# Chunk 0 of a windowed attention with a two-layer network: scales of w_in found for two blocks at once instead of one

## The chip, the cores and the metric

One core of one Trainium2 chip runs the whole program. The metric is the device time of one execution in microseconds (us); three runs of the kernel before gave 936.11, 936.60 and 936.64 us, median 936.6.

## What is computed

Eight batches with eight heads, 576 positions and 64 channels go through causal attention with a window of 128 positions and a linear bias per head. The result, laid out as 4608 tokens by 512 channels, goes through two matrix products with a gate between them:

```python
scores = where((rel >= 0) & (rel < 128), q @ k.T / sqrt(64) - slope * abs(rel), -1e9)
attn = exp(scores - max(scores)); attn = attn / (sum(attn) + 1e-9)
x = (attn @ v).transpose(0, 2, 1, 3).reshape(4608, 512)
h = x @ w_in                                   # w_in 512 x 2048
g = where(h >= 1, h, where(h <= -1, 0, (h + 1) ** 2 / 4))
out = g @ w_out                                # w_out 2048 x 512
```

## The kernel before

The 4608 tokens are cut into 12 chunks of 384 (`CH`); a chunk has four pairs of heads (`p`, four a chunk). The columns of `w_in` and the rows of `w_out` are cut into 16 blocks of 128 (`fc`). For each chunk `c` and each block `fc`, `layer1` multiplies the chunk's `x` by block `fc` of `w_in` into a PSUM bank `h`, ScalarE makes `u` from it (L666), VectorE makes `g` (L667, L668), and `layer2`, two blocks later (`LAG`), adds `g` times the block of `w_out` to three accumulators `acc` (L688 in chunk 0, L691 to L693 in the others). Attention of later chunks is woven between these steps: `scores` (PE, tiles `s`), `soften` (VectorE L537, ScalarE L539, tiles `z`), sums and weights on GpSimd (L549, L550, tiles `ep`), `weights_t` (PE transposes, tiles `p`) and `values` (tiles `x`).

Numbers in fp32 are multiplied as two fp16 halves, high and low. So each block of `w_in` needs a power of two as its scale before it can be split. In chunk 0 this is done on the way, block by block:

- `fetch_weights` loads block `fc` of both matrices into one of three buffers `raw`; `unfold` (ScalarE L190, L191) and `float32_of` (VectorE L195) make them fp32 (`f_i` for w_in, `wf` for w_out). `convert_in` also reduces `f_i` to its largest magnitude per row (L204), `convert_out` does it for `wf` on ScalarE (L229).
- `scale_in` calls `scale_of`: PE spreads the column of row maxima over all partitions (`across`, L160, tile `m_i`), VectorE reduces it to one number (L167) and makes the power of two and its inverse by three operations on one column (L169, L170, L171), into `i_in` and `s_in`.
- `split_in` makes one more column operation (`fall_in`, L212) and then the halves of the block: ScalarE the high half (L220), VectorE the low one (L221), both named `wi`.

Which block is converted and which is scaled and split after which step `f` of layer 1 stands in two tables by hand, `CONVERT` and `SPLIT`; where a table has no entry, `f + 5` is converted and `f + 4` is split. The order on each engine is then set by the tile framework's scheduler, which works from the order of the code and the dependences it finds; each engine runs its own instructions strictly in that order.

The buffers that matter here: `h` has two PSUM banks (`ps_h`), the accumulators three, and all short-lived PSUM tiles (`s`, `p`, `x`, `m_i`) share three banks (`ps_a`). `f_i` has three buffers, `raw` three.

Of the kernel before, what the change touches and what calls it, by code (L numbers as in the profile page):

```python
# [15 lines left out]
ALU = mybir.AluOpType  # L16
# [4 lines left out]
def windowed_attention_then_ffn(  # L21
# [21 lines left out]
    V, S, G, T, DMA = nc.vector, nc.scalar, nc.gpsimd, nc.tensor, nc.sync  # L43
# [17 lines left out]
    X = mybir.AxisListType.X  # L61
# [15 lines left out]
    def bank(name):  # L77
        return ps_a.tile([P, 4 * P], F32, name=name, tag="ps_a")
# [61 lines left out]
    s_in = const.tile([P, NFC], F32, name="s_in")  # L140
    i_in = const.tile([P, NFC], F32, name="i_in")
# [3 lines left out]
    s_x, i_x, fall, gain, half, shift, o_g = {}, {}, {}, {}, {}, {}, {}  # L145
    tops, diag = {}, {}
    s_q, s_k, z_of, s_2, i_2 = {}, {}, {}, {}, {}

    def column(name, tag, bufs=2, n=1):
        return ap1.tile([P, n], F32, name=name, tag=tag, bufs=bufs)  # L150

    def spread(name, rows):

        diag[name] = rows

    def across(b, rows):

        r = rows.bitcast(BF16)
        for a in range(rows.shape[1]):
            T.matmul(b[:, a * P:(a + 1) * P], r[:, 2 * a + 1:2 * a + 2].broadcast_to([P, P]), ident16, start=True, stop=True)  # L160

    def scale_of(name, s, i):

        b = bank(f"m_{name}")[:, :P]
        across(b, diag.pop(name))
        top = column(f"top_{name}", "top")
        V.tensor_reduce(top, b, X, ALU.max)  # L167
        ti = top.bitcast(I32)
        V.tensor_scalar(ti, ti, 0x7F800000, None, ALU.bitwise_and)  # L169
        V.tensor_scalar(i, top, 2.0 ** -100, 1.0 / TOP, ALU.max, ALU.mult)  # L170
        V.reciprocal(s, i)  # L171
# [7 lines left out]
    def fetch_weights(fc):  # L179
        w = raw[fc] = rawp.tile([P, 2, DM, 2], I32, name=f"raw{fc}", tag=f"raw{fc % 3}")  # L180
        if 0 < fc < 3:
            G.memset(w[:1, :, 0, :1], 0)
        DMA.dma_start(w[:, 0].rearrange("p (c f) w -> p c f w", c=NCC),
                      wi32[:, 2 * fc * P:2 * (fc + 1) * P].rearrange("(c p) (f w) -> p c f w", p=P, w=2))
        DMA.dma_start(w[:, 1], wo32[fc * P:(fc + 1) * P, :].rearrange("p (f w) -> p f w", w=2))

    def unfold(fc, which=slice(0, 2)):

        low, high = raw[fc][:, which, :, 0], raw[fc][:, which, :, 1]
        S.activation(high.bitcast(F32), high.bitcast(F32), AF.Prelu, scale=2.0 ** -112, alpha=2.0 ** 32)  # L190
        S.activation(low, low.bitcast(U32), AF.Copy, scale=0.9375 * 2.0 ** -29)  # L191

    def float32_of(fc, a, out):

        V.scalar_tensor_tensor(out.bitcast(I32), raw[fc][:, a, :, 1], 3, raw[fc][:, a, :, 0], ALU.logical_shift_left, ALU.bitwise_or)  # L195

    wide, rows_i = {}, {}

    def convert_in(fc):
        f = wide[fc] = wp.tile([P, DM], F32, name=f"f_i{fc}", tag="f_i", bufs=3)  # L200
        unfold(fc)
        float32_of(fc, 0, f)
        rows = column(f"rows_i{fc}", "rows", 4)
        V.tensor_reduce(rows, f, X, ALU.max, apply_absolute_value=True)  # L204
        spread(f"i{fc}", rows)

    def scale_in(fc):
        s1, i1 = s_in[:, fc:fc + 1], i_in[:, fc:fc + 1]
        scale_of(f"i{fc}", s1, i1)

    def fall_in(fc):
        V.tensor_scalar(fall[0][:, fc:fc + 1], i_in[:, fc:fc + 1], i_x[0], 0.25, ALU.mult, ALU.mult)  # L212

    def split_in(fc):
        if fc > 1:
            fall_in(fc)
        f, s1 = wide.pop(fc), s_in[:, fc:fc + 1]
        t = wp.tile([P, 2, DM], F16, name=f"wi{fc}", tag=f"wi{fc}")
        wi[fc] = t.rearrange("p s (c f) -> p s c f", c=NCC)
        S.activation(t[:, 0], f, AF.Copy, scale=s1)  # L220
        V.scalar_tensor_tensor(t[:, 1], f, s1, t[:, 0], ALU.mult, ALU.subtract)  # L221
# [4 lines left out]
    def convert_out(fc):  # L226
        wf[fc] = wp.tile([P, DM], F32, name=f"wf{fc}", tag=f"wf{fc}")
        float32_of(fc, 1, wf[fc])
        S.activation(junk, wf[fc], AF.Abs, accum_out=rows_o[:, fc:fc + 1])  # L229

    def scale_out(stage):
        if stage == 0:
            V.tensor_reduce(rows_o[:, NFC:], rows_o[:, :NFC], X, ALU.max)
            spread("o", rows_o[:, NFC:])
        else:
            scale_of("o", s_out, i_out)
            V.tensor_reduce(reach, i_in, X, ALU.max)
            V.tensor_scalar(reach, reach, float(NCC * P) * TOP * TOP * 1.001, None, ALU.mult)
# [561 lines left out]
    for i in range(NCHUNK * NFC + LAG):  # L800
        c, fc = divmod(i, NFC)
        ops = []
        if c < NCHUNK:
            if i == 0:
                ops += [lambda g=g: split_x(0, g, xn.pop((0, g))) for g in range(NPAIR)]
            if c == 0 and fc == 0:

                ops.append(lambda: behind([last_x[0]], lambda: layer1(0, 0)))
            else:
                ops.append(lambda c=c, fc=fc: layer1(c, fc))  # L810
            if c == 0:
                ops.append(lambda fc=fc: convert_after(fc))
            if c == 0 and fc == NFC - 2:
                ops.append(lambda: scale_out(0))
            if c == 0 and fc == NFC - 1:
                ops.append(lambda: scale_out(1))
            if c == 1:
                ops.append(lambda c=c, fc=fc: behind(done_g[c, fc - 1] if fc else [], lambda: split_out(fc)))
            if fc == NFC - 1 and c + 1 < NCHUNK:
                ops.append(lambda c=c: scales(c + 1))  # L820
        ffn.append(ops)
        ops = []
        if i >= LAG:
            ops.append(lambda i=i: layer2(*divmod(i - LAG, NFC)))
        if c == 0:
            ops.append(lambda fc=fc: split_after(fc))
        ffn.append(ops)

    def convert_after(f):

        for fc in CONVERT.get(f, (f + 5,)):
            if fc < NFC:
                if fc + 2 < NFC:
                    fetch_weights(fc + 2)
                behind(done_g[f], lambda: convert_in(fc))
                behind(done_g[f], lambda: convert_out(fc))
        for fc in SPLIT.get(f, (f + 4,)):
            if fc < NFC:
                behind(done_g[f], lambda: scale_in(fc))

    def split_after(f):

        for fc in SPLIT.get(f, (f + 4,)):
            if fc < NFC:
                behind(done_g[f], lambda: split_in(fc))

    CONVERT = {0: (3,), 1: (4, 5), 2: (6,), 3: (7, 8)}
# [6 lines left out]
    def convert_early(t):  # L854
        m = EARLY[t]
        fc, second = divmod(t, 2)
        if not second:
            behind(done_t[m], lambda: fetch_weights(fc + 2))
        behind(done_t[m], lambda: (convert_out if second else convert_in)(fc))

    then = {4: [lambda: reach_of_v(0), lambda: reach_of_v(1)], 5: [lambda: scale_in(0), lambda: reach_of_v(2), lambda: reach_of_v(3)],
            6: [lambda: split_in(0), lambda: scale_x(0)], 7: [lambda: scale_in(1)],
            8: [lambda: split_in(1), lambda: fall_in(0), lambda: fall_in(1)]}
    keep_busy(KEEP[0])

# [59 lines left out]
```

## Time and profile before

| | |
|---|---|
| runs | 936.11, 936.60, 936.64 us |
| the profiled execution | 935.53 us |
| its span on the core | 933.8 us |
| PE / VectorE / ScalarE / GpSimd busy over the span | 97% / 73% / 68% / 24% |
| granted TensorE clock, mean | 0.992 of 2.4 GHz |

A busy share of PE is not a share of its peak: a matmul's record overlaps the next one's, so the tables of waits and the starts of neighbouring matmuls say more than the share. Engines are named PE (TensorE), DVE (VectorE), ACT (ScalarE) and POOL (GpSimd), and SP is the queue that issues most transfers. Chunk 0 runs from about 41 to 138 us of the span.

### The profile page before, as it was taken

What the parts mean: (1) busy time and instruction counts of PE and PEld (TensorE: products, weight loads), DVE (VectorE), ACT (ScalarE), POOL (GpSimd) and SP (SyncE); (2) the same over time, 40 slices, a digit from 0 to 9 for tenths busy, and PEclk for the clock granted to TensorE, in tenths of its full rate; (3) what the DMA queues carried; (4) which work ended last, traced back from release to release, by engine and by line L of the source; (5) the groups of instructions that cost most, each with busy time, mean ns of one, the idle gap of its engine ahead of it and who ended that gap; (6) DMA issues with size and microseconds to landing.
All of it is one profiled execution on the core that took longest, in us unless ns stands there. A gap on an engine that the chain in (4) does not pass through costs nothing.

```text
span 933.8 us, 18976 instructions
## 1 busy us (share of the span) xinstructions
PE 907.0 (97%) x6661; PEld 501.7 (54%) x6661; DVE 684.6 (73%) x2070; ACT 637.5 (68%) x1668; POOL 220.5 (24%) x298
## 2 busy tenths in 40 slices
PE   9789999999999999999999999999999999999997
PEld 6344554554555555555555555555555555555553
DVE  6889979988877876877877777777877867653332
ACT  5889958888677766676776677677677657643332
POOL 6332221211122212212222221221222221222221
PEclk9889999999999999999999999999999999999999
DMA  7657723444544343334344334424532412320001
GB/s 242 218 177 255 244 63 95 81 96 117 102 106 116 77 87 89 95 97 100 100 93 94 94 78 94 116 66 103 119 75 46 102 36 35 76 48 15 34 1 35
DMA packets 178736, 91.41 MB, mean 98 GB/s; under 512 B 128848, under 2 KB 168016, under 8 KB 178640
## 3 DMA queue, kind: packets, MB, share of 16 engines
q1 hardware_dynamic: 178496, 90.07, 38.8%
q8 instruction: 52, 0.85, 0.4%
q14 instruction: 44, 0.36, 0.1%
q10 hardware_dynamic: 144, 0.13, 0.0%
HBM read 49.28 MB, written 9.44 MB: 63 GB/s over the span
## 4 chain that ended last, share of the span: by engine, by line
PE 66%; DVE 18%; ACT 10%; issue 3%; DMA 1%; POOL 1%; DVEq 0%; SPq 0%; ACTq 0%; POOLq 0%
PE h L659 10%; PE h L660 10%; PE h L661 10%; PE acc L691 9%; PE acc L693 9%; PE acc L692 9%; PE x L629 3%; DVE g L667 3%; PE s L490 3%; PE acc L688 2%; ACT hl L585 2%; ACT z L511 2%; DVE g L668 2%; ACT u L666 2%; DVE z L509 2%
## 5 line engine op out<-in xcount | busy, mean ns | idle before, releaser
L676 POOL TENSOR_TENSOR gl<-g,gh 128x384 f16<-128x384 f32 x176 | 170.2, 968 | 608.6 <-ACT gh L675 552.6
L667 DVE SCALAR_TENSOR_TENSOR g<-u,half 128x384 f32<-128x384 f32 x176 | 112.0, 636 | 175.3 <-ACT u L666 172.6
L691 PE MATMUL acc<-wo,gh 128*128 128x512 f16 x528 | 200.4, 380 | 1.2 <-ACT o L704 1.1
L692 PE MATMUL acc<-wo,gh 128*128 128x512 f16 x528 | 200.1, 379 | 0.0
L693 PE MATMUL acc<-wo,gl 128*128 128x512 f16 x528 | 184.6, 379 | 0.3 <-POOL gl L676 0.3
L666 ACT ACTIVATE u<-h,shift,fall 128x384 f32<-128x384 f32 x176 | 115.8, 667 | 98.2 <-PE h L661 97.4
L675 ACT CAST gh<-g 128x384 f16<-128x384 f32 x176 | 89.6, 509 | 122.0 <-DVE g L668 111.3
L659 PE MATMUL h<-x,wi 128*128 128x384 f16 x384 | 125.3, 326 | 2.1 <-DVE g L668 1.7
L659 PE MATMUL h<-xh,wi 128*128 128x384 f16 x384 | 125.1, 326 | 2.2 <-DVE g L668 1.9
L660 PE MATMUL h<-x,wi 128*128 128x384 f16 x384 | 125.1, 326 | 0.5 <-DVE x L639 0.5
L660 PE MATMUL h<-xl,wi 128*128 128x384 f16 x384 | 125.2, 326 | 0.0
L661 PE MATMUL h<-x,wi 128*128 128x384 f16 x384 | 125.2, 326 | 0.0
L661 PE MATMUL h<-xh,wi 128*128 128x384 f16 x384 | 124.9, 326 | 0.0
L511 ACT ACTIVATE z<-z,nmax 128x192 f32<-128x192 f32 (+2 forms) x240 | 102.5, 430 | 16.8 <-DVE nmax L509 16.7
L668 DVE SCALAR_TENSOR_TENSOR g<-h,gain,g 128x384 f32<-128x384 f32 x176 | 108.4, 616 | 4.3
L660 PEld LDWEIGHTS <-wi 128*128 128x128 f16 x768 | 75.1, 98 | 62.7 <-issue 10.9
L659 PEld LDWEIGHTS <-wi 128*128 128x128 f16 x768 | 75.1, 98 | 58.9 <-issue 2.9
L661 PEld LDWEIGHTS <-wi 128*128 128x128 f16 x768 | 75.1, 98 | 51.2 <-issue 0.9
L586 DVE SCALAR_TENSOR_TENSOR hl<-z,rc,hl 128x192 f16<-128x192 f32 (+2 forms) x240 | 85.9, 413 | 7.5 <-ACT hl L585 6.6
L585 ACT ACTIVATE hl<-z,rc 128x192 f16<-128x192 f32 (+2 forms) x240 | 83.5, 430 | 3.5 <-DVE rc L518 2.4
L509 DVE CUSTOM_DVE_ANT_0 z<-s,near,z_of 128x192 f32<-128x192 f32 (+2 forms) x240 | 82.2, 393 | 3.6 <-PE s L490 3.5
L693 PEld LDWEIGHTS <-gl 128*128 128x128 f16 x528 | 51.6, 98 | 61.3 <-POOL gl L676 0.8
(159 smaller groups left out, 1221.4 us busy)
## 6 DMA issues: line engine op xcount, KB each, us to landing
out_dram<-o SPq DMA_DIRECT2D x35, 256.0 KB, 2.3
raw<-in_moe_w_in_dram SPq DMA_DIRECT2D x16, 512.0 KB, 4.5
raw<-in_moe_w_out_dram SPq DMA_DIRECT2D x16, 512.0 KB, 5.4
vn<-in_v_dram SPq DMA_DIRECT2D x32, 256.0 KB, 3.2
qk<-in_q_dram SPq DMA_DIRECT2D x40, 192.0 KB, 2.4
qk<-in_k_dram SPq DMA_DIRECT2D x28, 256.0 KB, 2.8
vn<-in_v_dram SPq DMA_DIRECT2D x16, 192.0 KB, 2.8
qk<-in_k_dram SPq DMA_DIRECT2D x12, 192.0 KB, 2.5
```

The lines of the kernel that those rows point to most:

```text
L511: d = S.activation(z[:, i, c0:KW], z[:, i, c0:KW], AF.Exp, bias=nmax[:, i:i + 1], scale=-1.0, accum_out=sm[:, i, 0:1])
L585: S.activation(hl[:, 0, i, w], z[:, i, c0:KW], AF.Copy, scale=rc[:, i:i + 1])
L659: T.matmul(ph, wi[fc][:, 0, cc, :], xh, start=(cc == 0), stop=False)
L660: T.matmul(ph, wi[fc][:, 0, cc, :], xl, start=False, stop=False)
L661: last_mm[0] = T.matmul(ph, wi[fc][:, 1, cc, :], xh, start=False, stop=(cc == NCC - 1)).ins
L666: first = S.activation(u, ph, AF.Relu, bias=shift[c] if c else quarter, scale=fall[c][:, col])
L667: V.scalar_tensor_tensor(g, u, half[c] if c else 0.5, u, ALU.min, ALU.mult)
L668: last = V.scalar_tensor_tensor(g, ph, gain[c][:, col] if c else fall[c][:, col], g, ALU.mult, ALU.max)
L676: G.tensor_tensor(gl, g, gh, ALU.subtract)
L691: T.matmul(a, gh[:, ts], wo[fc][:, 0], start=first, stop=False)
L692: T.matmul(a, gh[:, ts], wo[fc][:, 1], start=False, stop=False)
L693: last_mm[0] = T.matmul(a, gl[:, ts], wo[fc][:, 0], start=False, stop=last).ins
```

## The change

From block 2 on, an even block and the odd one after it share one `rows` tile of two columns, one `across` of two matmul passes into 256 columns, and one chain (reduce, mask, scale, reciprocal, `fall`) on two columns. The chain is therefore made when both blocks are converted, and both are split one after the other. `CONVERT` moves block 7 one step earlier (from step 3 to step 2); `SPLIT` now has an entry for each pair, at steps 0, 2, 3, 5, 7, 9 and 11. Blocks 0 and 1 are as before.

```diff
     def scale_of(name, s, i):
-        b = bank(f"m_{name}")[:, :P]
+        n = s.shape[1]
+        b = bank(f"m_{name}")[:, :n * P]
         across(b, diag.pop(name))
-        top = column(f"top_{name}", "top")
-        V.tensor_reduce(top, b, X, ALU.max)
+        top = column(f"top_{name}", "top", 2, n)
+        V.tensor_reduce(top, b.rearrange("p (a w) -> p a w", w=P), X, ALU.max)
...
         float32_of(fc, 0, f)
-        rows = column(f"rows_i{fc}", "rows", 4)
-        V.tensor_reduce(rows, f, X, ALU.max, apply_absolute_value=True)
-        spread(f"i{fc}", rows)
+        if fc < 2 or fc % 2 == 0:
+            diag[f"i{fc}"] = column(f"rows_i{fc}", "rows", 4, 1 if fc < 2 else 2)
+        rows = diag[f"i{fc}" if fc < 2 else f"i{fc - fc % 2}"]
+        V.tensor_reduce(rows[:, fc % 2 if fc > 1 else 0:][:, :1], f, X, ALU.max, apply_absolute_value=True)
 
     def scale_in(fc):
-        s1, i1 = s_in[:, fc:fc + 1], i_in[:, fc:fc + 1]
-        scale_of(f"i{fc}", s1, i1)
+        n = 1 if fc < 2 else 2
+        if fc < 2 or fc % 2 == 0:
+            scale_of(f"i{fc}", s_in[:, fc:fc + n], i_in[:, fc:fc + n])
 
     def fall_in(fc):
-        V.tensor_scalar(fall[0][:, fc:fc + 1], i_in[:, fc:fc + 1], i_x[0], 0.25, ALU.mult, ALU.mult)
+        n = 1 if fc < 2 else 2
+        V.tensor_scalar(fall[0][:, fc:fc + n], i_in[:, fc:fc + n], i_x[0], 0.25, ALU.mult, ALU.mult)
 
     def split_in(fc):
-        if fc > 1:
+        if fc > 1 and fc % 2 == 0:
             fall_in(fc)
...
-        for fc in SPLIT.get(f, (f + 4,)):
+        for fc in SPLIT.get(f, ()):
...
-    CONVERT = {0: (3,), 1: (4, 5), 2: (6,), 3: (7, 8)}
-    SPLIT = {0: (2,), 1: (3,), 2: (4, 5), 3: (6,), 4: (7, 8)}
+    CONVERT = {0: (3,), 1: (4, 5), 2: (6, 7), 3: (8,)}
+    SPLIT = {f: (n, n + 1) for f, n in zip((0, 2, 3, 5, 7, 9, 11), range(2, NFC, 2))}
```

The scheduler then places many instructions of chunk 0 and of the first third of chunk 1 anew. Line numbers of the changed kernel are 1 higher from L167, 3 higher from L204 and 4 higher from L212 on. Three places matter for the prediction.

**Place 1: the high halves of blocks 2 and 3 on ACT, early in chunk 0.** `wi2` and `wi3` are the high halves of the blocks, `z_10` and `z_11` the exponentials of the two heads of pair 5, `u_0_2` what follows layer 1 of block 2. Before:

```order
L229 ACTIVATE junk_159,rows_o_158<-wf5_737 128x512
L220 ACTIVATE wi2_693<-f_i2_540,s_in_153 128x512
L220 ACTIVATE wi3_768<-f_i3_614,s_in_153 128x512
L539 ACTIVATE z_10_754,sums_134<-z_10_754,nmax_10_755 128x256 x2
L539 ACTIVATE z_11_761,sums_134<-z_11_761,nmax_11_762 128x256 x2
L666 ACTIVATE u_0_2_804<-h_0_2_791,quarter_91,fall0_510 128x384
```

With the change:

```order
L233 ACTIVATE junk_159,rows_o_158<-wf5_739 128x512
L543 ACTIVATE z_10_749,sums_134<-z_10_749,nmax_10_750 128x256 x2
L543 ACTIVATE z_11_756,sums_134<-z_11_756,nmax_11_757 128x256
L441 ACTIVATE lus_160<-lus_160,qscale_97 128x384
L543 ACTIVATE z_11_756,sums_134<-z_11_756,nmax_11_757 128x256
L543 ACTIVATE z_11_756,sums_134<-z_11_756,nmax_11_757 128x192
L543 ACTIVATE z_10_749,sums_134<-z_10_749,nmax_10_750 128x192
L224 ACTIVATE wi2_693<-f_i2_540,s_in_153 128x512
L224 ACTIVATE wi3_696<-f_i3_614,s_in_153 128x512
L670 ACTIVATE u_0_2_795<-h_0_2_782,quarter_91,fall0_510 128x384
```

Six exponentials and the scaling of a query tile, all behind the scores of pair 5, now stand ahead of `wi2`.

The same place on PE, with `s_10` and `s_11` the scores of pair 5, `m_i` the spread row maxima and `h_0_2` layer 1 of block 2. Before:

```order
L160 MATMUL m_i3_740<-ident16_151,rows_i3_618 128x128
L462 MATMUL s_11_0_748<-kr_5_458,lus_160 128x256
L462 MATMUL s_10_0_747<-kr_5_458,lus_160 128x256
L462 MATMUL s_11_0_748<-kr_5_458,lus_160 128x256
L462 MATMUL s_10_0_747<-kr_5_458,lus_160 128x256
L659 LDWEIGHTS wi2_693
```

With the change:

```order
L466 MATMUL s_11_0_743<-kr_5_458,lus_160 128x256
L466 MATMUL s_10_0_742<-kr_5_458,lus_160 128x256
L466 MATMUL s_11_0_743<-kr_5_458,lus_160 128x256
L466 MATMUL s_10_0_742<-kr_5_458,lus_160 128x256
L160 LDWEIGHTS rows_i2_544
L160 MATMUL m_i2_622<-ident16_151,rows_i2_544 128x128
L466 MATMUL s_11_2_763<-kr_5_458,lus_160 128x192
L466 MATMUL s_10_2_762<-kr_5_458,lus_160 128x192
L160 LDWEIGHTS rows_i4_726
L160 MATMUL m_i4_823<-ident16_151,rows_i4_726 128x128
L160 LDWEIGHTS rows_1_688
L160 MATMUL m_x1_851<-ident16_151,rows_1_688 128x128
L663 LDWEIGHTS wi2_693
```

The scores now come ahead of the spreading of the row maxima (two passes), so the chain that gives `s_in` starts behind them.

**Place 2: PE behind layer 1 of blocks 10 and 11.** `p_14`, `p_15` are transposes of attention weights that POOL has just made, `x_7` the values of pair 7. The rows of before are those around the same transposes:

```order
L688 MATMUL acc_0_0_839<-wf11_1125,g_0_11_1439 128x512
L559 MATMUL p_14_1363<-ident_85,ep_14_1276 128x128 x3
L160 LDWEIGHTS rows_i14_1312
L160 MATMUL m_i14_1397<-ident16_151,rows_i14_1312 128x128
L559 MATMUL p_15_1404<-ident_85,ep_15_1283 128x128 x3
L688 MATMUL acc_0_1_840<-wf11_1125,g_0_11_1439 128x512
```

With the change:

```order
L665 MATMUL h_0_11_1365<-xh_0_3_589,wi11_1170 128x384
L160 LDWEIGHTS rows_i12_1143
L160 MATMUL m_i12_1265<-ident16_151,rows_i12_1143 128x128
L563 MATMUL p_14_1315<-ident_85,ep_14_1224 128x128 x3
L563 MATMUL p_15_1348<-ident_85,ep_15_1231 128x128 x3
L160 LDWEIGHTS rows_i14_1260
L160 MATMUL m_i14_1383<-ident16_151,rows_i14_1260 128x128
L692 MATMUL acc_0_0_835<-wf10_1005,g_0_10_1336 128x512
```

Before, layer 1 of blocks 12 and 13 and 2.3 rounds of layer 2 stood between block 11 and `p_14`; now `p_14` follows block 11, and blocks 12 and 13 come after both transposes.

**Place 3: DVE at the end of chunk 0.** `g_0_14` at L668 is the last reader of the PSUM bank that `h_1_0`, the first layer 1 of chunk 1, is written to; `vs`, `h_8`, `h_9` and `wo0` are low halves of values, queries and keys, and w_out. Before:

```order
L667 SCALAR_TENSOR_TENSOR g_0_14_1568<-u_0_14_1567 128x384
L371 TENSOR_SCALAR s_k2_1491<-i_q2_1487,s_22_1545 128x4
L376 TENSOR_SCALAR near_133<-near_133,s_22_1545 128x192
L423 TENSOR_SCALAR r2_2747<-r2_2747 128x1
L668 SCALAR_TENSOR_TENSOR g_0_14_1568<-h_0_14_1554,fall0_510,g_0_14_1568 128x384
L445 SCALAR_TENSOR_TENSOR vs_8_1763<-vn_8_993,s_22_1545,vs_8_1763 128x512
```

With the change:

```order
L250 SCALAR_TENSOR_TENSOR wo0_1633<-wf0_403,s_out_155,wo0_1633 128x512
L390 SCALAR_TENSOR_TENSOR h_8_1521<-qk_8_961,s_k2_1435,h_8_1521 128x512
L431 TENSOR_SCALAR half2_2695<-u2_2692 128x1
L432 TENSOR_SCALAR shift2_2696<-u2_2692 128x1
L436 TENSOR_SCALAR o_g2_2694<-o_g2_2694,i_out_156 128x1
L433 TENSOR_SCALAR fall1_850<-i_in_154,i_x1_849,shift1_1558 128x16
L390 SCALAR_TENSOR_TENSOR h_9_1751<-qk_9_971,s_k2_1435,h_9_1751 128x512
L671 SCALAR_TENSOR_TENSOR g_0_14_1512<-u_0_14_1511 128x384
L434 TENSOR_SCALAR gain1_1555<-fall1_850,half1_1557 128x16
L671 SCALAR_TENSOR_TENSOR g_0_15_1540<-u_0_15_1539 128x384
L672 SCALAR_TENSOR_TENSOR g_0_14_1512<-h_0_14_1498,fall0_510,g_0_14_1512 128x384
```

Three `vs`, `wo0`, `h_8` and `h_9`, six operations of 512 columns, now stand ahead of `g_0_14`; before, they stood behind it or, `wo0`, much later.

## Rows read from the trace of the kernel before

**Rows 1.** The profile's page: busy time of each engine over the span, and the granted clock by 40 equal slices.

```profile
PE 907.0 (97%) x6661; PEld 501.7 (54%) x6661; DVE 684.6 (73%) x2070; ACT 637.5 (68%) x1668; POOL 220.5 (24%) x298
PEclk9889999999999999999999999999999999999999
```

**Rows 2.** Busy time by stretch; columns: stretch, its length, then busy us and instructions of PE, weight loads, DVE, ACT and POOL, granted clock, DMA share, GB/s.

```profile
70.00:95.00 25.00, 23.34 (x108) 11.96 (x105) 22.60 (x67) 22.41 (x47) 6.06 (x13) 1.00 0.75 264
95.00:120.00 25.00, 25.00 (x133) 13.55 (x132) 24.12 (x73) 22.70 (x46) 9.50 (x15) 1.00 0.70 222
120.00:145.00 25.00, 24.68 (x145) 13.03 (x144) 18.35 (x74) 13.91 (x30) 3.71 (x10) 1.00 0.22 64
```

**Rows 3.** Timeline of PE: the starts at which it waited between 60 and 164 us; columns: start, length, engine, line, operation, tiles, shape, count, and in brackets the idle time and what ended it.

```profile
65.28 2.84 PE L688 MATMUL acc<-wf,g 128*128 128x512 f32 x6 [0.19 <-DVE g L668]
68.96 0.23 PE L160 MATMUL m_i<-ident,rows_i 128*128 128x128 bf16 x1 [0.84 <-DVE rc L545]
70.83 2.84 PE L688 MATMUL acc<-wf,g 128*128 128x512 f32 x6 [0.19 <-DVE g L668]
78.69 0.23 PE L160 MATMUL m_i<-ident,rows_i 128*128 128x128 bf16 x1 [0.36 <-DVE rows_i L204]
80.03 0.32 PE L659 MATMUL h<-xh,wi 128*128 128x384 f16 x1 [1.11 <-DVE g L668]
138.16 0.32 PE L659 MATMUL h<-x,wi 128*128 128x384 f16 x1 [0.32 <-DVE g L668]
163.31 0.90 PE L629 MATMUL x<-lus,vs 128*64 128x256 f16 x14 [1.83 <-DVE rc L517]
```

**Rows 4.** Waits of PE between 200 and 270 us: who waited for whom, us in total, times, longest.

```profile
PE acc L691 <- ACT o L704: 1.1, 1, 1.1
PE h L659 <- DVE g L668: 1.0, 2, 0.6
PE h L660 <- DVE x L639: 0.5, 1, 0.5
```

**Rows 5.** Timelines around place 1, PE first, then ACT, then DVE; columns as in rows 3.

```profile
58.38 0.22 PE L160 MATMUL m_i<-ident,rows_i 128*128 128x128 bf16 x1
58.53 1.13 PE L462 MATMUL s<-kr,lus 64*128 64x256 f32 x8
59.59 0.34 PE L659 MATMUL h<-xh,wi 128*128 128x384 f16 x1
...
61.65 0.59 PE L462 MATMUL s<-kr,lus 64*128 64x192 f32 x2
...
56.99 0.71 ACT L220 ACTIVATE wi<-f_i,s_in 128x512 f16<-128x512 f32 x1
...
57.73 0.75 DVE L221 SCALAR_TENSOR_TENSOR wi<-f_i,s_in,wi 128x512 f16<-128x512 f32 x1 [1.06 <-ACT wi L220]
```

**Rows 6.** Groups of instructions between 50 and 145 us; columns: line, engine, operation, tiles, shape, count, then busy us and the mean ns of one, then the idle time before them.

```profile
L537 DVE CUSTOM_DVE_ANT_0 z<-s,rel 128x256 f32<-128x256 f32 x6 | 2.5, 420 | 0.0
L537 DVE CUSTOM_DVE_ANT_0 z<-s,rel 128x192 f32<-128x192 f32 x6 | 2.0, 354 | 0.5 <-PE s L462 0.4
L539 ACT ACTIVATE z<-z,nmax 128x256 f32<-128x256 f32 x12 | 5.9, 495 | 0.0
L539 ACT ACTIVATE z<-z,nmax 128x192 f32<-128x192 f32 x6 | 2.7, 450 | 0.6 <-DVE nmax L537 0.6
L437 ACT ACTIVATE lus<-lus,qscale 128x384 f32<-128x384 f32 x2 | 1.2, 616 | 1.6 <-PE s L462 1.6
L167 DVE TENSOR_REDUCE top_i<-m_i 128x1 f32<-128x128 f32 x14 | 3.8, 283 | 0.0
L366 DVE TENSOR_REDUCE i<-m 128x2 f32<-128x256 f32 x1 | 0.4, 418 | 0.0
L169 DVE TENSOR_SCALAR top_i<-top_i 128x1 int32<-128x1 int32 x14 | 2.0, 147 | 0.0
L170 DVE TENSOR_SCALAR i_in<-top_i 128x1 f32<-128x1 f32 x14 | 1.9, 146 | 0.1
L171 DVE RECIPROCAL s_in<-i_in 128x1 f32<-128x1 f32 x14 | 2.0, 156 | 0.2
L212 DVE TENSOR_SCALAR fall<-i_in,i_x 128x1 f32<-128x1 f32 x14 | 2.6, 196 | 0.0
L445 DVE SCALAR_TENSOR_TENSOR vs<-vn,s,vs 128x512 f16<-128x512 f32 x3 | 2.1, 741 | 0.0
```

**Rows 7.** Granted clock: a stretch at the lower level (columns as in rows 2), and what PE waited for as the level fell (columns as in rows 3).

```profile
48.20:54.90 6.70, 5.23 (x10) 2.52 (x11) 6.70 (x14) 6.70 (x10) 1.96 (x4) 0.50 0.21 62
...
49.08 1.69 PE L559 MATMUL p<-ident,ep 128*128 128x128 f32 x6 [2.71 <-POOL ep L550]
```

**Rows 8.** Timeline around place 2: ACT and DVE idle in chunk 0's last quarter, POOL ahead of `p_14`; columns as in rows 3.

```profile
123.08 0.67 ACT L666 ACTIVATE u<-h,quarter,fall 128x384 f32<-128x384 f32 x1 [3.85 <-PE h L661]
...
123.78 0.56 DVE L667 SCALAR_TENSOR_TENSOR g<-u 128x384 f32<-128x384 f32 x1 [3.15 <-ACT u L666]
...
116.65 2.02 POOL L549 TENSOR_TENSOR z<-z 128x384 f32<-128x384 f32 x2 [8.14 <-ACT z L539]
118.74 1.93 POOL L550 TENSOR_TENSOR ep<-z,rc 128x384 f32<-128x384 f32 x2
```

More of the change, by code (lines that the diff above doesn't have):

```diff
@@ L841, in split_after @@
     def split_after(f):
-        for fc in SPLIT.get(f, (f + 4,)):
+        for fc in SPLIT.get(f, ()):
             if fc < NFC:
                 behind(done_g[f], lambda: split_in(fc))
-    CONVERT = {0: (3,), 1: (4, 5), 2: (6,), 3: (7, 8)}
-    SPLIT = {0: (2,), 1: (3,), 2: (4, 5), 3: (6,), 4: (7, 8)}
+    CONVERT = {0: (3,), 1: (4, 5), 2: (6, 7), 3: (8,)}
+    SPLIT = {f: (n, n + 1) for f, n in zip((0, 2, 3, 5, 7, 9, 11), range(2, NFC, 2))}
     EARLY = (2, 3, 4, 5, 6, 7)
```

## Prediction, before the changed kernel was run

> **What bounds the kernel now.** I read the busy shares first: PE is busy for 97% of the span, VectorE (DVE) for 73%, ScalarE (ACT) for 68% [rows 1]. So only what PE waits for, or the speed at which it runs, can move the time by much. The clock line beside them shows full speed but for two early slices [rows 1]. Then I read the stretches of chunk 0, which is all that the change rewrites: DVE is busy for 22.6 and 24.1 of 25 us, ACT for 22.4 and 22.7, and PE, at full clock, for 23.3 and 25.0 [rows 2]. All three are nearly full there, and one can't tell from shares who holds up whom. The starts at which PE waits decide it: in chunk 0 behind 60 us there are six, 0.19, 0.84, 0.19, 0.36, 1.11 and 0.32 us, 3.0 us together, and one of 1.83 early in chunk 1 [rows 3]. DVE ended all of them, but they are all the time that PE can win back there. Between 200 and 270 us a further 1.1 + 1.0 + 0.5 = 2.6 us of waits stand [rows 4].
>
> The profiled execution took 935.5 us, the median of the runs is 936.6: sums are made against the profile, and 1.1 us is added at the end. A difference under 0.2% (1.9 us) can't be told from none.
>
> **What it removes.** A pair saves one reduce, one mask, one scale, one reciprocal and one `fall`, 35 instructions over seven pairs. By durations a pair gives back 2 x 0.283 - 0.418 (the reduce of 2x128 that stands elsewhere in the kernel) + 0.147 + 0.146 + 0.156 + 0.196 = 0.79 us [rows 6], 5.6 us of DVE in all. A record's length contains time that overlaps the next one, so this is the upper end. The lower end is nothing for what lies in a dependent chain, where a second column was done while the first chain's results were on their way; half, 2.8 us, is what I take for DVE's own time. For PE I price it at nothing where DVE waits for somebody else: at the first pair it does (below), and in the last quarter of chunk 0 DVE stands idle for 3.15 us and ACT for 3.85 us, waiting for PE [rows 8]. If that cover is gone, it is worth at most the waits named above.
>
> The Trainium skill ("Perfetto Trace Analysis", section Optimizing Scalar/DVE Operations) puts a fixed cost of about 60 ns on a DVE instruction that reads SBUF and about 125 ns on one that reads PSUM, and says that grouping helps where the engine is saturated. By it the saving would be an estimated 28 x 0.06 + 7 x 0.125 = 2.6 us of DVE; the sum goes by the rows.
>
> **Place 1, the first pair.** Before, ACT splits block 2 from 56.99 to 57.70, DVE makes the low half by 58.48, and layer 1 of block 2 (`h_0_2`) starts at 59.59, right behind the scores that start at 58.53, without a wait [rows 5]. Now the spreading of the row maxima stands behind those scores. I walk it: the scores start where `m_i3` stood, at 58.38, and take 59.59 - 58.53 = 1.06 us, to 59.4; two passes of `m_i2` end at about 59.7. DVE has the softening of pair 5 and the chain on its list, and ACT has six exponentials and the scaling of the query tile ahead of `wi2`. The first exponential can start one softening (0.42) after the scores, at 60.1; four exponentials of 0.495, two of 0.45 and the scaling of 0.616 make 3.5 us [rows 6]; then the high half at 0.71 [rows 5] ends at 64.3. So `h_0_2` starts at 64.3 where it started at 59.6, 4.7 us later. Between stand only the 192-column scores (0.59 [rows 5]), `m_i4` and a share of `m_x1`, 0.9 to 1.1 us: PE waits for **+3.6** more. Bounds: 3.1 if ACT's neighbours overlap, 4.0 if the low half queues too. DVE's saving is worth nothing here, since it is ACT's list that is late.
>
> **The clock.** In the profile of before the granted clock was 0.50 from 48.2 to 54.9 us, that is 1.2 instead of 2.4 GHz, and PE had waited 2.71 us at 49.08 and had been idle ahead of it too [rows 7]. The new wait at place 1 is longer than that one. If the clock falls behind it for the same 6.7 us, PE does half the work in it and loses 3.35; if not, nothing. Nearest row: the fall beside a wait of 2.7. I take a fall, and **+2.3**, since about 1 us of it is time in which PE would have waited for the next splits anyway.
>
> **Old waits between 65 and 81 us.** PE comes to them 3 to 6 us later, and what it waited for there (`g`, `rc`, `rows_i` of DVE) is not behind the late split, so they go: 0.19 + 0.84 + 0.19 + 0.36 + 1.11 [rows 3], **-2.7**. Ends: 0 and -2.7.
>
> **Place 2, behind block 11.** `p_14` and `p_15` wait for POOL's two sums and two weightings, 2.02 + 1.93 = 3.95 us of work that starts at 116.65 in before and ends at 120.7 [rows 8]. Before, layer 1 of blocks 12 and 13 and rounds of layer 2 stood ahead of `p_14`; now PE comes to it right behind block 11. POOL can't start sooner by as much, as its exponentials and the reciprocals `rc` stand behind the row maxima of block 12 and of `x_1` on DVE. Adding up the new lists from the previous common point, PE is through with block 11 at 118.7 and POOL with the last weighting at 121.0, on the clock of before. Bounds 0 (POOL moves up with it) and 3.95 (PE waits for all four); I take **+2.3**. Queued behind the waiting transposes is layer 2 of block 10, so nothing covers it. DVE's and ACT's own idle time of 3 us [rows 8] shrinks by it, which costs nothing.
>
> **Place 3, the end of chunk 0.** Layer 1 of chunk 1 writes a bank whose last reader is `g_0_14`. Six low halves of 512 columns now stand ahead of it, 0.74 us each [rows 6], 4.4 us in all; PE has about half of that in other work before it (layer 2 of blocks 13 and 14, pieces of attention). With the old wait of 0.32 [rows 3] gone in it, **+2.0**; bounds 0 and 4.4.
>
> **Later.** These low halves are then done early, so the wait of 1.83 at 163.31 for `rc` [rows 3] loses its reason: **-1.8** (ends 0 and -1.8). Of the 2.6 us of waits behind 200 us [rows 4] a PE that is some 6 us late finds half made: **-1.3** (ends 0 and -2.6). SP issues the same transfers; the one that refills the buffer of block 5 waits for `f_i5`, now some 7 us later, and no wait of PE in [rows 3] was put down to a transfer, so I cost that at nothing; its cover is the weaving of the attention, and without it place 2 would grow.
>
> **Sum:** 3.6 + 2.3 - 2.7 + 2.3 + 2.0 - 1.8 - 1.3 = +4.4, so 939.9 for the profile and **941.0** for the median.
>
> **A rule for the same point.** The same section of the Trainium skill says that where Scalar and Vector aren't saturated but cause bubbles on other engines, instructions broken up may let work end sooner. That is this change read backwards. The trace agrees as to before: with single columns `h_0_2` waited for nothing [rows 5].
>
> **Rivals.**
> 1. *DVE is the bound in chunk 0, and its saved time comes through* (the other side). For it: 24.1 of 25 us busy [rows 2], and DVE ends every wait of PE behind 60 us [rows 3]. Then the 3.0 us of chunk 0 and the 1.83 go: 936.6 - 4.8 = 931.8. It decides if the first pair's wait stays under about 1 us, that is if `wi2` comes out ahead of the exponentials at run time. Against: each engine keeps its list's order, and the list has them ahead. 0.15.
> 2. *No fall of the clock.* All as forecast without the 2.3: 938.7. For it: at 49 us more than one wait came together, at place 1 it is one. 0.23.
> 3. *Nothing is given back.* The fall at its full 3.35, the later 1.3 not absorbed: 941.0 + 1.05 + 1.3 = 943.4. For it: behind 200 us PE has had some waits for ACT's `o` [rows 4] which a shift of all engines together leaves as they are. 0.12.
>
> **How the numbers follow.** The forecast has 0.50, with its own range of 938.5 to 943.0 from the bounds of places 2 and 3, of which 0.08 may fall under 938.5. Slower: 0.42 of it, 0.11 of rival 2 and the 0.12 of rival 3, 0.65. Within 0.2%: 0.08 + 0.12 of rival 2 + 0.02 of rival 1, 0.22. Faster: 0.13. The range, 935.5 to 944.5, leaves out nearly all of rival 1 and a little at the top.
>
> **What would show it.** Right: `h_0_2` starts near 64 instead of 59.6 with a wait of 3 to 4 us for ACT's `wi`; a stretch at clock 0.50 within the next 10 us; a wait of `p` for POOL's `ep` near 120; a wait of `h` for `g` near 145 in place of 0.32; the 1.83 of `x` gone; 35 DVE instructions fewer. Wrong: a wait at place 1 under 1 us with the clock at 1.00 throughout (rival 1), or PE waits behind 92 us that sum to what they were.

## The result, and the profile after

Five runs of the change gave 940.99 to 942.41 us, median 941.58; five of before gave a median of 936.6. The ratio is 1.0059 (95% interval 1.0049 to 1.0070): slower by 5.5 us (4.6 to 6.6) by the ratio, by 5.0 between the medians. The forecast was 941.0, range 935.5 to 944.5, slower. The profiled execution took 942.41 us with a span of 940.7, 6.9 us over the span of before.

The page of the change, busy times and granted clock, beside [rows 1]:

```profile
PE 913.2 (97%) x6661; PEld 503.1 (53%) x6661; DVE 685.9 (73%) x2035; ACT 638.5 (68%) x1668; POOL 221.5 (24%) x298
PEclk9689999999999999999999999999999999999999
```

35 VectorE instructions fewer, and VectorE is busy for 1.3 us more. The chains take 2.7 us less (9.6 against 12.3, below), but other instructions take longer: the 16 conversions to `f_i` last 0.84 us each where they lasted 0.72, 1.7 us in all, in both profiles of either kernel. Why they do is open. TensorE's work is the same, and the span is longer.

The starts at which PE waited for over 0.15 us between 58 and 165 us, columns as in [rows 3]:

```profile
62.21 0.93 PE L466 MATMUL s<-kr,lus 64*128 64x192 f32 x4 [0.82 <-DVE top_i L168]
66.16 0.34 PE L663 MATMUL h<-xh,wi 128*128 128x384 f16 x1 [2.37 <-ACT wi L224]
67.75 0.50 PE L665 MATMUL h<-xh,wi 128*128 128x384 f16 x1 [0.16 <-DVE wi L225]
72.76 2.84 PE L692 MATMUL acc<-wf,g 128*128 128x512 f32 x6 [0.33 <-DVE g L672]
85.00 2.84 PE L692 MATMUL acc<-wf,g 128*128 128x512 f32 x6 [0.22 <-DVE g L672]
100.95 2.84 PE L692 MATMUL acc<-wf,g 128*128 128x512 f32 x6 [0.46 <-DVE g L672]
123.94 0.55 PE L563 MATMUL p<-ident,ep 128*128 128x128 f32 x3 [1.83 <-POOL ep L554]
124.72 0.83 PE L563 MATMUL p<-ident,ep 128*128 128x128 f32 x3 [0.24 <-POOL ep L554]
125.99 3.95 PE L692 MATMUL acc<-wf,g 128*128 128x512 f32 x6 [0.26 <-DVE g L672]
139.13 2.84 PE L692 MATMUL acc<-wf,g 128*128 128x512 f32 x6 [0.17 <-DVE g L672]
150.51 0.32 PE L663 MATMUL h<-x,wi 128*128 128x384 f16 x1 [0.96 <-DVE g L672]
```

ScalarE at place 1:

```profile
61.85 0.51 ACT L543 ACTIVATE z<-z,nmax 128x256 f32<-128x256 f32 x1 [3.04 <-DVE nmax L541]
...
65.40 1.32 ACT L224 ACTIVATE wi<-f_i,s_in 128x512 f16<-128x512 f32 x2
```

The six exponentials and the query's scaling run from 61.85 to 65.40 without a gap, and only then `wi2`. At place 1 `h_0_2` waits 2.37 us for `wi2` of ScalarE, at place 2 the transposes wait for POOL's `ep`, at place 3 `h_1_0` waits for `g_0_14`. The wait of 1.83 at 163.31 has no row any more. Between 200 and 280 us, beside [rows 4] (the stretch is longer at its end, since the same matmuls come 7.5 to 9.5 us later here):

```profile
PE h L663 <- DVE g L672: 1.0, 2, 0.6
PE acc L695 <- ACT o L708: 0.4, 1, 0.4
```

Stretches of the change at the lower clock, 1.2 GHz, columns as in [rows 2]:

```profile
25.90:42.60 16.70, 13.18 (x51) 6.70 (x53) 14.24 (x50) 13.13 (x30) 5.33 (x10) 0.50 0.72 249
53.10:56.60 3.50, 3.50 (x5) 1.42 (x6) 3.50 (x7) 3.50 (x6) 0.22 (x1) 0.51 0.29 83
66.80:70.80 4.00, 3.84 (x14) 1.63 (x15) 3.96 (x4) 0.01 (x1) 2.82 (x4) 0.57 0.00 0
124.90:128.60 3.70, 3.44 (x8) 1.67 (x8) 3.70 (x11) 2.54 (x8) 3.06 (x8) 0.55 0.56 189
```

The third stretch lies behind the wait of place 1, the fourth behind that of place 2. The first two begin ahead of the first instruction that the change moves on any engine (54.12, on VectorE); the second stands where before has the stretch of [rows 7], and is shorter.

### The profile page after: what moved, and what is told of

The parts are those of the page before. It is cut to its first block, busy times and chain, and to the rows that moved or that the text cites. A ratio compares the mean times of both kernels' runs of the same rounds, so it can differ in the third digit from the quotient of the medians.

```text
span 940.7 us, 18940 instructions
## 1 busy us (share of the span) xinstructions
PE 913.2 (97%) x6661; PEld 503.1 (53%) x6661; DVE 685.9 (73%) x2035; ACT 638.5 (68%) x1668; POOL 221.5 (24%) x298
## 4 chain that ended last, share of the span: by engine, by line
PE 64%; DVE 18%; ACT 13%; issue 3%; POOL 1%; DMA 0%; DVEq 0%; ACTq 0%; SPq 0%; POOLq 0%
PE h L663 10%; PE h L665 10%; PE h L664 10%; PE acc L695 9%; PE acc L696 9%; PE acc L697 9%; PE x L633 3%; DVE g L671 3%; ACT hl L589 3%; PE s L494 2%; DVE g L672 2%; ACT z L515 2%; ACT u L670 2%; DVE z L513 2%; PE acc L692 2%
```

## The experiments

The theory: TensorE is held up at named places, because the order of the lists was changed; a wait in place 1 or 2 also brings down the clock; VectorE's saved time is worth nothing there. Each ratio below is to runs of before on the same chip.

| run | us | ratio, 95% interval |
|---|---|---|
| e1, pairs from block 4 on | 939.1 | 1.0021 (1.0011 to 1.0030) |
| e2, first pair alone | 940.98 | 1.0054 (1.0037 to 1.0071) |
| e3, single columns, new tables | 936.88 | 1.0000 (0.9992 to 1.0009) |
| e4, pairs, first split at step 1 | 938.67 | 1.0022 (1.0012 to 1.0032) |
| e5, place 1 filled with matmuls | 945.68 | 1.0094 (1.0080 to 1.0109) |
| e6, saved time put back | 943.04 | 1.0069 (1.0056 to 1.0082) |
| e7, pairs split a step earlier | 935.73 | 0.9998 (0.9990 to 1.0007) |
| e8, as e4, last two pairs earlier | 937.16 | 1.0015 (1.0007 to 1.0024) |
| e9, before again, one run | 936.32 | |
| e10, the change again, one run | 946.35 | |
| e11, the change, last two pairs earlier | 940.98 | 1.0048 (1.0035 to 1.0062) |
| e12, the chain by single columns | 943.87 | 1.0070 (1.0056 to 1.0084) |

### Which part of the change costs the time: e1 and e2

e1 keeps blocks 2 and 3 single:

```diff
-        n = 1 if fc < 2 else 2
+        n = 1 if fc < 4 else 2
...
-    SPLIT = {f: (n, n + 1) for f, n in zip((0, 2, 3, 5, 7, 9, 11), range(2, NFC, 2))}
+    SPLIT = {0: (2,), 1: (3,), **{f: (n, n + 1) for f, n in zip((2, 3, 5, 7, 9, 11), range(4, NFC, 2))}}
```

> Blocks 2 and 3 keep single columns and steps 0 and 1; pairs from block 4 on, at the steps of the change. TensorE's list is that of before up to block 3 and that of the change from block 4 on. Theory (place 1 and the clock behind it carry most of the loss): h_0_2 waits for nothing near 59.6 us, the clock stays at full speed behind it, places 2 and 3 stay: 936.5 to 938.0, some 4 to 5 us under the change. Rival (the loss is made at places 2 and 3): 940 to 941.5, as the change. Rival (saved VectorE time is worth something once place 1 is out of the way): under 935.

e2 pairs blocks 2 and 3 alone:

```diff
-        n = 1 if fc < 2 else 2
+        n = 1 if fc not in (2, 3) else 2
...
+    SPLIT = {0: (2, 3), 1: (), 2: (4, 5), 3: (6,), 4: (7, 8)}     # and f + 4 behind, CONVERT of before
```

> Only blocks 2 and 3 are a pair, at step 0; all others single, by the tables of before. Theory: place 1 waits as in the change (2.4 us for wi of ScalarE, with what lies around it 3.5), the clock falls for some 4 us behind it, places 2 and 3 are as before: 939 to 941. Rival (places 2 and 3 carry the loss): 936 to 937.5.

The wait of place 1 is there in e2 as in the change, with the row that PE waits at first:

```profile
61.52 0.93 PE L466 MATMUL s<-kr,lus 64*128 64x192 f32 x4 [0.82 <-DVE top_i L168]
65.47 0.34 PE L663 MATMUL h<-xh,wi 128*128 128x384 f16 x1 [2.71 <-ACT wi L224]
```

and in e1 it is gone, while those of places 2 and 3 stand:

```profile
120.92 0.55 PE L563 MATMUL p<-ident,ep 128*128 128x128 f32 x3 [1.84 <-POOL ep L554]
...
146.54 0.32 PE L663 MATMUL h<-x,wi 128*128 128x384 f16 x1 [0.96 <-DVE g L672]
```

One pair of seven costs 5.1 us by e2's ratio; the other six cost 2.0 by e1's. Together that is 1.6 more than the 5.5 that the change loses by its ratio. The intervals would allow no difference, but e1's trace shows a wait and a stretch at the lower clock that neither before nor the change has:

```profile
72.86 0.86 PE L563 MATMUL p<-ident,ep 128*128 128x128 f32 x3 [2.09 <-POOL ep L554]
```

```profile
72.90:76.40 3.50, 3.50 (x7) 1.95 (x8) 3.19 (x5) 3.47 (x10) 1.42 (x3) 0.51 0.07 25
```

In the change TensorE is late enough from place 1 to come to these transposes at 77.24 without a wait. So part of what is late at place 1 covers what would be late behind. e1 was expected under 938.0, with the clock at full speed behind `h_0_2`; it is 1.1 over, and this wait and this fall are what I had not listed. e2's time came out as expected, but its place 3 is not as before: `h_1_0` waits 1.36 us there.

### Pairing or the steps: e3 and e4

e3 is the kernel before with both tables of the change; e4 is the change with `CONVERT` of before and the pairs at other steps:

```diff
-    SPLIT = {f: (n, n + 1) for f, n in zip((0, 2, 3, 5, 7, 9, 11), range(2, NFC, 2))}
+    SPLIT = {f: (n, n + 1) for f, n in zip((1, 2, 4, 5, 7, 9, 11), range(2, NFC, 2))}
```

> Both tables of the change, but every block by a column of its own, with the 35 small operations back. Theory (the place of the split decides, not the number of small operations): wi2 and wi3 stand ahead of the exponentials of pair 5, so no wait at place 1; 936 to 939, faster than the change. Rival (the saved small operations are worth their 3 us of VectorE, and the steps cost what the change costs): 943 to 945.

> All pairs kept, CONVERT as before, the first pair's split at step 1 and the third's at step 4; by the list the spread row maxima of blocks 2 and 3 then stand ahead of the scores of pair 5, and the tail from block 4 on is the change's. Theory: no wait of h_0_2 for ScalarE over 1 us, so 936.5 to 938.5 with all the pairs. Rival (a pair's chain costs its wait wherever it stands, since the first block waits for the second's conversion): 940 to 942, with the wait moved to another place.

e3 takes what before takes (1.0000). It is not the change's list with single columns, though: the scheduler orders it anew from about 39 us on. `h_0_2` waits for nothing, as expected, but the layers 1 of blocks 3 and 4 wait 0.95 and 1.64 us for `wi`, while the transposes that wait 2.71 us at 49.08 in before come at 61.49 without that wait and no fall of the clock stands there. So e3 shows that the new tables needn't cost time, not that they have no part in the change's order.

In e4 the pair's row maxima are spread ahead of the scores, and `h_0_2` starts right behind the scores, without a wait, where the change waits 2.37:

```profile
59.56 0.34 PE L663 MATMUL h<-xh,wi 128*128 128x384 f16 x1
```

A wait of 0.70 for `wi` stands at 72.48, at block 4, and one of 1.73 for `g` at 96.66, where the change waits 0.46. e4 lies just above its bound and 2.1 us over before: place 1 is cheap there, place 2 stands as in e1. So not the pair as such costs the 3 us at place 1, but where its chain stands.

### The clock at place 1: e5

```diff
+        if c == 0 and fc == 2:
+            for _ in range(16):
+                behind([scored_at[NPAIR + 1]], lambda: T.matmul(ph, wi[1][:, 0, 0, :], xs[0][0][0], start=True, stop=True))
```

> The change, with 16 matmuls of 384 columns more (2.6 us) behind the last scores of pair 5, into the bank of h_0_2, which is written over; all lists else as in the change. TensorE is busy for most of the wait for wi2. Theory (the wait itself stays, the clock behind it need not fall): granted clock 1.00 from 60 to 75 us, some 1.5 to 2 us less lost there, 939.5 to 940.5. Rival (the clock falls all the same, or what is won is waited away by 92 us): 941 to 942.5.

Waits of PE and stretches in e5:

```profile
65.33 0.34 PE L666 MATMUL h<-xh,wi 128*128 128x384 f16 x1 [0.21 <-ACT wi L224]
71.23 1.98 PE L695 MATMUL acc<-wf,g 128*128 128x512 f32 x4 [0.82 <-DVE g L675]
102.21 4.22 PE L695 MATMUL acc<-wf,g 128*128 128x512 f32 x6 [2.50 <-DVE g L675]
```

```profile
60.00:70.00 10.00, 8.38 (x50) 4.46 (x47) 7.88 (x26) 6.02 (x17) 4.43 (x5) 1.00 0.23 77
70.00:80.00 10.00, 9.18 (x45) 4.59 (x43) 8.35 (x22) 9.46 (x15) 0.43 (x1) 1.00 0.61 210
102.70:107.10 4.40, 4.40 (x11) 2.04 (x10) 4.30 (x8) 0.87 (x3) 0.00 (x0) 0.61 0.12 28
127.00:135.00 8.00, 7.50 (x16) 2.97 (x16) 6.74 (x15) 6.20 (x17) 3.99 (x9) 0.57 0.66 218
```

The mechanism is right: with TensorE kept busy the clock stays at 1.00 where it stood at 0.57. The time is wrong by 5 us and more. The layer 2 that starts at 72.76 in the change starts at 71.23 here, 1.5 us earlier; 0.8 of that was there before place 1 (the transposes `p_8` start at 49.86 against 50.69), so about 0.7 is what the clock gave back, since PE now waits 0.82 for `g` in place of 0.33. By the layer 2 that starts at 97.65 in the change that is gone: it starts at 96.87 here, 0.8 earlier, as `p_8` does. Behind it e5 loses: a wait of 2.50 for `g`, a fall of the clock there, and a longer one at place 2. What made that `g` late is in part below, at e12; why the fall at place 2 is longer I have not settled.

### Is VectorE's saved time worth anything: e6

```diff
+    spare = const.tile([P, 1], F32, name="spare")
+    V.memset(spare, 1.0)
...
         V.reciprocal(s, i)
+        for _ in range(5 if n == 2 else 0):
+            V.tensor_scalar(spare, spare, 1.0, None, ALU.mult)
```

> The change, with five column operations on an unused column behind each pair's reciprocal, so that the 35 VectorE instructions are back and the lists are else the same. Theory (the saved VectorE time is worth nothing for TensorE): 941 to 942.5, as the change. Rival (it is worth its 3 to 5 us, and the change would be slower still without it): 944 to 946.

35 instructions of 0.148 us put 5.2 us back on VectorE, with all lists else unchanged. The ratio rises from 1.0059 to 1.0069; the intervals overlap, so the difference is somewhere between nothing and 2.5 us. The rival's 3 to 5 us are excluded; "nothing" is not shown by the ratios. Two profiles come closer. In those of e6 and of the change's second run (e10, below) the stretches at the lower clock stand at the same times, at 28 to 45, 52 to 59, 66 to 72 and 127 to 134 us, `h_0_2` starts at 67.58 and 67.62, `h_1_0` at 154.18 in both, and the spans are 944.5 and 944.6 us. With the clock alike, 35 instructions more cost TensorE nothing that one execution of each can show.

### Only the places: e7, e8 and e11

e7 splits the pairs at steps 0, 1, 2, 4, 6, 8 and 10; e8 is e4, and e11 the change, with the last two pairs at 8 and 10:

```diff
-    SPLIT = {f: (n, n + 1) for f, n in zip((0, 2, 3, 5, 7, 9, 11), range(2, NFC, 2))}
+    SPLIT = {f: (n, n + 1) for f, n in zip((0, 1, 2, 4, 6, 8, 10), range(2, NFC, 2))}     # e7
+    SPLIT = {f: (n, n + 1) for f, n in zip((1, 2, 4, 5, 7, 8, 10), range(2, NFC, 2))}     # e8
+    SPLIT = {f: (n, n + 1) for f, n in zip((0, 2, 3, 5, 7, 8, 10), range(2, NFC, 2))}     # e11
```

> All pairs, each from the third block pair on split one step earlier (0, 1, 2, 4, 6, 8, 10). By the list the row maxima of blocks 2 and 3 stand ahead of the scores of pair 5, and p_14 behind two layer 2 rounds and part of layer 1 of blocks 12 and 13. Theory (only the places of waits matter): neither place 1 nor place 2 waits over 0.5 us, 935.5 to 938. Rival (pairs cost 2 us wherever they stand): 938.5 to 940.

> As the kernel with all pairs and the first at step 1 (938.67), but the last two pairs are split one step earlier (8 and 10); the lists are the same up to block 9, then p_14 stands behind layer 2 of block 10 and p_15 behind part of layer 1 of blocks 12 and 13. Theory (what that kernel loses behind block 8, it loses at place 2): the wait for POOL's ep of 2.1 us shrinks under 0.7, 936.5 to 937.5. Rival (the loss behind block 8 is elsewhere, or the wait comes back at p_15 or at layer 2): 938 to 939.5.

> The change, with the last two pairs split one step earlier (8 and 10): the lists are the change's up to block 9, place 1 stands, p_14 comes behind layer 2 of block 10. Theory (place 2 costs its wait and the fall of the clock behind it): the wait for ep under 0.7, no fall near 127 us, 938 to 940. Rival (as in the kernel e8, what is won there is waited for again behind 140 us): 940.5 to 942.

e7, place 1 and behind block 8:

```profile
60.53 0.34 PE L663 MATMUL h<-xh,wi 128*128 128x384 f16 x1 [0.24 <-ACT wi L224]
...
139.29 0.32 PE L663 MATMUL h<-x,wi 128*128 128x384 f16 x1 [0.50 <-DVE g L672]
```

With all seven pairs and neither place waiting, the kernel takes what before takes (0.9998): in this order the pairs cost nothing and give nothing, to within 0.9 us by the interval. e8 and e11 take the wait for `ep` away, and another comes in its place. e11 behind 105 us:

```profile
138.57 2.84 PE L692 MATMUL acc<-wf,g 128*128 128x512 f32 x6 [0.64 <-DVE g L672]
150.72 0.27 PE L494 MATMUL s<-h 64*64 64x192 f16 x2 [1.72 <-DVE nmax L513]
151.31 0.68 PE L494 MATMUL s<-h 64*64 64x192 f16 x22 [0.32 <-DVE nmax L513]
152.75 0.48 PE L663 MATMUL h<-x,wi 128*128 128x384 f16 x1 [0.77 <-DVE g L672]
```

The wait of 2.3 us at place 2 has become one of 2.0 for the softening of chunk 2's scores at 150 us. Both things that the theory asked of e11's trace hold, no wait for `ep` over 0.7 and the clock at 1.00 from 126 to 150 us, and the time is still the rival's 940.98. (The profiled execution of e11 took 944.81 us, the other four 940.6 to 941.5: its rows show where TensorE waits, not what the median takes.) e8 (1.0015 against e4's 1.0022) can't be told from e4, though it lies in the range I gave.

### What belongs to the run: e9 and e10

Both kernels as they are, profiled a second time.

> The kernel before, profiled a second time. Its lists up to about 45 us are those of the change word for word. Theory (the 1.6 us by which the change was late at p_8, 50.7 against 49.1, and the clock's fall from 26 to 42 us instead of 31.5 to 38 come from run to run and not from the change): the stretch at the lower clock ahead of 45 us differs from that of the first profile by over 2 us, and p_8 starts 0.5 to 1.5 us later than 49.1. Rival (the change makes it): the same stretch and the same 49.1.

> The change, profiled a second time. Theory: the wait for wi2 of 2.4, that for POOL's ep of 1.8, that for g of 1.0 stand as in the first profile, while the stretches at the lower clock begin or end elsewhere by over 1 us; place 1 costs a fall in both. Rival: the falls are the same to 0.2 us, and so part of the program.

The change's second profile, waits at the three places and the stretches behind the first two:

```profile
67.62 0.50 PE L663 MATMUL h<-xh,wi 128*128 128x384 f16 x1 [2.36 <-ACT wi L224]
...
125.78 0.55 PE L563 MATMUL p<-ident,ep 128*128 128x128 f32 x3 [1.84 <-POOL ep L554]
...
154.18 0.32 PE L663 MATMUL h<-x,wi 128*128 128x384 f16 x1 [0.95 <-DVE g L672]
```

```profile
65.10:72.10 7.00, 4.50 (x15) 1.65 (x15) 5.44 (x13) 3.08 (x9) 4.42 (x5) 0.54 0.23 66
127.50:133.90 6.40, 6.14 (x9) 2.14 (x8) 5.31 (x12) 5.20 (x15) 2.89 (x7) 0.50 0.61 197
```

The waits agree to 0.01 us. The falls stand at the same places, but the stretches last 7.0 and 6.4 us (at 0.54 and 0.50 in the mean) where they lasted 4.0 and 3.7 (at 0.57 and 0.55), and the one behind `p_8` lasts 6.8 instead of 3.5; the span is 944.6 instead of 940.7. By the starts of the same matmuls the second run is 0.65 us late at `p_8`, 1.5 at the scores of pair 5, 1.8 at the layer 2 behind place 1 (74.60 against 72.76) and 3.7 behind place 2 (142.81 against 139.13). So runs of one and the same program differ by some 4 us, most of it through the length of the falls; the longer one at place 1 cost only 0.4 of that. Ahead of the change's first moved instruction the expectation held in part: in before's second profile the early stretch begins some 5 us sooner, as expected, but `p_8` starts at 49.45, only 0.4 later; in the change it starts at 50.69 and 51.34, in e1, e2 and e5 at 49.9 to 50.0, in e11 at 51.90. That spread at lists that are the same is not the order's doing. Whether the 1.6 us by which the change came late to `p_8` are more than chance stays open.

### Single and double columns against GpSimd: e12

```diff
-        V.tensor_scalar(ti, ti, 0x7F800000, None, ALU.bitwise_and)
+        for a in range(n):
+            V.tensor_scalar(ti[:, a:a + 1], ti[:, a:a + 1], 0x7F800000, None, ALU.bitwise_and)     # scale and fall alike
```

> The change, with the mask, the scale and the fall of a pair made as two instructions of one column each (21 VectorE instructions more; reduce, spread and reciprocal stay on two columns). In the change one such instruction on two columns lasted up to 0.98 us, while GpSimd ran its sums; single columns never lasted over 0.21. Theory (two columns wait for GpSimd, one column doesn't): none over 0.25 us. Rival (what stalls them is something ahead of them on VectorE or a write they need): 0.4 to 1.0 us again. For the time both expect 940.5 to 943, since VectorE's time is not what place 1 and place 2 wait for.

The chain in the change between 50 and 145 us, columns as in [rows 6]:

```profile
L168 DVE TENSOR_REDUCE top_i<-m_i 128x2 f32<-128x256 f32 x7 | 2.9, 416 | 0.4 <-PE m_i L160 0.4
L216 DVE TENSOR_SCALAR fall<-i_in,i_x 128x2 f32<-128x2 f32 x7 | 2.6, 370 | 0.0
L170 DVE TENSOR_SCALAR top_i<-top_i 128x2 int32<-128x2 int32 x7 | 1.5, 209 | 0.0
L171 DVE TENSOR_SCALAR i_in<-top_i 128x2 f32<-128x2 f32 x7 | 1.5, 208 | 0.0
L172 DVE RECIPROCAL s_in<-i_in 128x2 f32<-128x2 f32 x7 | 1.1, 161 | 0.1
```

and in e12:

```profile
L219 DVE TENSOR_SCALAR fall<-i_in,i_x 128x1 f32<-128x1 f32 x14 | 2.7, 201 | 0.0
L173 DVE TENSOR_SCALAR i_in<-top_i 128x1 f32<-128x1 f32 x14 | 1.5, 147 | 0.0
L171 DVE TENSOR_SCALAR top_i<-top_i 128x1 int32<-128x1 int32 x14 | 1.5, 144 | 0.0
```

Seven `fall` of two columns take 2.6 us, as long as fourteen of one: half of the instructions, nothing saved. The mean hides two kinds; in the change one of them lasts from 97.87 to 98.85, beside POOL's sum:

```profile
97.87 0.98 DVE L216 TENSOR_SCALAR fall<-i_in,i_x 128x2 f32<-128x2 f32 x1
```

```profile
97.83 1.97 POOL L553 TENSOR_TENSOR z<-z 128x384 f32<-128x384 f32 x2 [10.54 <-ACT z L543]
```

The first of the two sums ends at 98.8, and so does the `fall`. In before, 16 masks, scales and `fall`s of one column ran beside work of POOL, and the longest took 0.20 us; in e12 15 did, and none took over 0.22. The theory holds. In e5 the mask and the scale of one pair met POOL's sums at 97.6 us and took 0.97 and 0.93 us; `g` stands behind them on VectorE, and its layer 2 is the one that waited 2.50. That is 0.8 us more than the one `fall` of 0.98 costs in the change, of the 1.3 us by which this `g` is done later than there. The time is 0.9 over what both theories gave; the list of e12 also differs from the change's behind 95 us in a few rows, so nothing is concluded from it but that 21 instructions more don't help.

The Trainium skill ("SBUF — State Buffer", section Who interferes with whom) states that a `tensor_scalar` can enter a mode in which it takes the port pair that VectorE shares with GpSimd, that whoever issues first holds the pair for the whole instruction, and that a `tensor_reduce` never does so on trn2. The rows agree: the reduce of two columns stayed within 0.43 us in all profiles, and the reciprocal within 0.17. That one column escapes the wait is what e12 shows here.

## Why the prediction was right, step by step

- **Place 1, +3.6.** Measured 0.82 + 2.37 + 0.16 = 3.35. ScalarE's list was walked rightly: `wi2` starts behind six exponentials and the query's scaling. `h_0_2` starts at 66.16 and not 64.3, since PE was already 1.6 late at `p_8`. The walk lets the softening begin when the passes of `m_i2` end (59.7) and not when the scores do (59.4); the first exponential came 1.76 us behind the first score where the walk has 1.72, so the slip did no harm. The 0.82 for the 192-column scores (the row says that they wait for `top_i`) I had not named; it is a piece of the same wait.
- **The clock, +2.3.** A fall came, a stretch of 4.0 us at 0.57 in one profile and of 7.0 at 0.54 in the other, against 6.7 at 0.50 forecast. Its worth was mis-sized: filled in, it gave 0.7 us by the next layer 2, not 2.3, and nothing by 97 us. And it was not the only one: a fall came behind place 2, which the sum did not have.
- **Old waits at 65 to 81, -2.7.** These five went; two of 0.33 and 0.22 came for them, so -2.1.
- **Place 2, +2.3.** 1.83 + 0.24 + 0.26 = 2.3, as summed. As what it costs in the end it was too high: taken away, a wait of 2.0 came behind it (e11).
- **Place 3, +2.0.** 0.96 in place of 0.32, +0.6: the sixth low half is done at 148.85 and TensorE comes at 149.55, so it waits for `g_0_14` alone. This is the largest single miss among the waits.
- **The 1.83 at 163 us, -1.8.** Gone. **Behind 200 us, -1.3:** 2.6 became 1.4, -1.2.
- **VectorE's saving, 2.8 us, worth nothing.** The two-column chains took 2.9 + 2.6 + 1.5 + 1.5 + 1.1 = 9.6 us against 12.3 of [rows 6], so 2.7 were saved; the size was right by luck: I had halved 5.6 for overlap within the chain, and what took part of it were the stalls beside POOL, which I had not seen. Its worth lies under 2.5 by the ratios, and at 0.1 between the two profiles with the same falls.

The waits summed as forecast make 3.6 - 2.7 + 2.3 + 2.0 - 1.8 - 1.3 = +2.1; measured they are 3.35 - 2.1 + 2.3 + 0.6 - 1.8 - 1.2, and 0.46 + 0.17 for two new ones, +1.8. The two falls behind places 1 and 2 took 4.0 us at 0.57 and 3.7 at 0.55, at most 1.7 + 1.7 = 3.4 us of work. With the 1.6 us at `p_8` that is 6.8; the same matmul starts at 280.03 in before and at 287.49 here, 7.5 later, so 0.7 is not accounted for, and the change wins back 0.6 behind it, to the 6.9 by which the profiled spans differ. The forecast had 2.1 + 2.3 = 4.4 and nothing for what comes ahead of place 1. What makes the clock fall at place 2 stays open: in e1 and e4 the same wait of 1.84 and 1.88 us for `ep` was followed by none. So the mechanism of places 1 and 2 is right, but that the total comes within 0.6 us of the median is in part luck: 1.4 too much for place 3 stands against a second fall and a late `p_8` that no term had. Nor do the places add, as e1's new wait and e11 show. Rival 1, VectorE as the bound, is out by the ratio; rival 2, no fall, by the stretches in both profiles; of rival 3, that later waits stay, the trace shows that about half of those behind 200 us go.

## What to carry to other kernels

Merging two short chains into one makes the first block wait for the second, so walk the list of the engine that uses the result and see what has slipped ahead of it; the instructions saved matter only if that engine was waited for. A wait taken away at one place came back at another three times here (e1, e8, e11), so measure a place by the kernel's time and not by its row. Where the clock can fall, a wait's price has a second part, which differs from run to run.

## What the runs showed of the hardware

- Masks, scales and `fall`s on two columns lasted up to 0.99 us beside GpSimd's work (e4), on one column never over 0.22, and two columns alone 0.16 to 0.21.
- The same program, with the same waits to 0.01 us at the three places, had stretches at a lower clock of 4.0 us (mean 0.57) and 7.0 us (mean 0.54) at one of them, and spans of 940.7 and 944.6 us.
- A wait of 1.83 to 1.88 us at the same transposes was followed by a fall of the clock in the change, e5, e6, e10 and e12, and by none in e1 and e4.
